# A pooled-attention and snake-activation kernel: the last two token units take two of their seven block products by a second level of Strassen, and GpSimd copies the output weight

## The chip, the cores and the metric

The kernel runs on one core of a Trainium2 chip, in float32 throughout. The metric is the device time of one execution in microseconds. Before the change three executions took 903.77, 904.64 and 906.18 us; their median is 904.64 us.

## The reference

```python
k_p = k.reshape(B, H, Sp, pool, D).mean(axis=3)      # B 8, H 8, S 576, D 64, pool 8
v_p = v.reshape(B, H, Sp, pool, D).mean(axis=3)
attn = softmax(scale * q @ k_p^T)                    # 1e-9 is added to the sum
x = (attn @ v_p).transpose(0, 2, 1, 3).reshape(4608, 512)
h = x @ w_in                                         # 512 x 2048
s = sin(alpha * h)
g = h + s * s / (alpha + 1e-9)
out = g @ w_out                                      # 2048 x 512
```

Nearly all of the arithmetic is in the two matrix products around the sine.

## The kernel before

**Units and groups.** The 4608 tokens are cut into nine units of 512. `run` walks them (u = 0 to 8) and calls `hidden(u, x)`, which makes h and g of one unit; in units 0 to 6 the attention of the next batch (batches 1 to 7) is woven in between. After the last unit, `outputs` computes the second product, eight batches one after the other. A unit has four groups (J = 0 to 3) of 512 hidden columns.

**The first product** is a 2 by 2 block Strassen scheme of seven products (Winograd's form). In the code product p multiplies `self.A[p]`, a block or a sum of blocks of `w_in` (`a..` are blocks, `as..` are sums), by a block of x (`xT`, tile `home0` to `home2`) or a difference of such blocks (`bt`, tile `home3`). One product of one group is `product(...)` at line 834: four matmuls of 128 rows, 128 weights and 256 columns, since two row tiles (`jj`) have two steps (`kk`) each. The trace has two records for each float32 matmul, so eight records for a product. The seven products of a group go in the order 1, 5, 6, 2, 7, 3, 4, and their intermediate sums are kept in four banks of PSUM: 1 goes into b1, ScalarE copies b1 to b6 (line 810), 5 goes into b5, which ScalarE copies out to the tile `p5`; 6 is added onto b6, ScalarE copies b6 to b7, 2 is added onto b1, 7 onto b7, 3 onto b6, 4 onto b7. In between VectorE adds `p5` to b7 and to b6 (line 809; the results are two quarters of the tile `h`), and product 4 may only go onto b7 when VectorE has read it.

**Sine and square.** `sin` (line 984) and `square` (line 991) run on ScalarE, per quarter of the group: quarter (0,0) comes from b1, (1,1) and (0,1) from the sums in `h`, (1,0) from b7 after product 4. `finish` (line 1036) adds the squares on VectorE, and `store_g` sends the group to the DRAM tensor `g_bridge`. The sines of the last two quarters, their squares and `finish` belong to the next group's time (`last_sines`, slots 0 to 2).

**The order is written by hand.** `hidden` has 28 slots to a unit, seven to a group, one for each product. `carry(u)` and `run` fill a list `x[slot]` of further work, and `extras` emits it in the middle of that slot. The five engines each take their instructions in the emitted order, so that a waiting instruction holds up all behind it on its engine.

**Inner products.** In units 1 to 6 three of the products of a unit (5 of groups 2 and 3, 1 of group 3) are themselves done by seven multiplications of 128 columns (`inner_product`, line 1014), in four steps a, b, d, e with two, two, one and two multiplications. After step a ScalarE copies the first result to both halves of a row tile (line 1018) and the second one to SBUF (line 1020); after step b it makes one copy inside the bank (line 1024); after step d VectorE adds the second result of step a (line 1029), and step e adds onto what VectorE wrote. Units 7 and 8 have none.

**The output weight.** In units 7 and 8 `load_w_out` brings `w_out` in and makes its own Strassen operands. It is a generator, and each `next(w)` in `run` is one piece: eight pieces of two ScalarE copies each (line 703), four pieces of four VectorE differences (line 712), five calls of `inner_w` of four VectorE differences each (line 730). In unit 7 the pieces are in slots 9 to 23, in unit 8 in slots 6, 10, 13, 14, 17 and 20. The last group of unit 8 also holds the first steps of `outputs` (slots 22, 25, 27): the first inner products of batch 0 with their VectorE sums (line 1267) and ScalarE copies (lines 1415, 1440).

Of the kernel before, what the change touches and what calls it, by code (L numbers as in the profile page):

```python
# [13 lines left out]
F32 = mybir.dt.float32  # L14
# [26 lines left out]
class Kernel:  # L41
# [637 lines left out]
    def load_w_out(self, wp):  # L679
# [4 lines left out]
        src = self.w_out.rearrange("(k p) n -> p k n", p=P)  # L684
        self.W = {}
        self.wb = {p: wp.tile([P, self.NJ, 2, 2, P], F32, name=f"wb{p}") for p in range(1, 8)}
        flat = lambda t: t[:].rearrange("p a b c d -> p (a b) (c d)")
        b11, b21, b22, t4, t1, t2, b12 = (flat(self.wb[p]) for p in range(1, 8))

# [8 lines left out]
        def put(i, k):  # L698

            for j, t in enumerate(((b11, b12), (b21, b22))[i]):  # L700
                yield
                for n in range(2):
                    nc.scalar.copy(out=t[:, k:k + 4, n * P:(n + 1) * P].rearrange("p k (a c) -> p k a c", a=4),
                                   in_=raw[i, k][:, :, j, :, n, :])
        yield from put(0, 0)
        yield from put(1, 0)
        for c in range(0, kk, 2):
# [9 lines left out]
            tt(t4, b21, t2)  # L717
            if c == 2:
                yield from put(1, 4)
        for p in (1, 2, 4, 6, 7):  # L720
            yield
            self.inner_w(p, wp)
        yield

    def inner_w(self, p, wp):
# [5 lines left out]
        if p in (4, 6, 7, 5):  # L731
            J = (4, 6, 7, 5).index(p)
            t1, t2, t4 = (self.A[i][:, :, J * JW * P:(J + 1) * JW * P].rearrange("p k (j d) -> p k j d", j=2) for i in (1, 2, 3))
        else:
            e = wp.tile([P, 3, 2, 2, P], F32, name=f"we{p}")
# [266 lines left out]
    def inner_product(self, G, p, ps, y):  # L1002
# [29 lines left out]
            products((3, 4), (c[1], c[2]))  # L1032
        return SimpleNamespace(a=a, b=b, d=d, e=e)

    def finish(self, Q, parts=(0, 1)):
        add = lambda o, x, y: self.nc.vector.tensor_tensor(out=o, in0=x, in1=y, op=OP.add)  # L1036
# [15 lines left out]

    def end_hidden(self):
        nc, Q = self.nc, self.group
        self.last_sines(Q, 2)
        self.squares(Q, 0)
        self.squares(Q, 1)
        self.finish(Q)
        self.store_g(Q)
# [405 lines left out]
    def run(self):  # L1465
        nc, tc = self.nc, self.tc
        pool = lambda s, n, b, **kw: s.enter_context(tc.tile_pool(name=n, bufs=b, **kw))
        with ExitStack() as top:
# [10 lines left out]
            with ExitStack() as one:  # L1479
# [35 lines left out]
                for u in range(self.NU):  # L1515
                    x = self.carry(u)
                    if u == self.B - 1:
                        att.close()
                        wo = pool(top, "wo", 1, side="right")
                        self.gp = pool(top, "gp", 1, side="right")  # L1520
                        w = self.load_w_out(wp=wo)
                        next(w)
                        for i in (9, 10, 12, 13, 15, 16, 17, 18, 20, 21, 23):
                            x[i].append(lambda: next(w))
                    elif u > self.B - 1:
                        homes.close()
# [12 lines left out]
            self.op = pool(top, "op", 1, reuse_waits="tile")  # L1539
# [39 lines left out]
```

## Time and profile before

The profiled execution spans 902.6 us from its first to its last instruction; the median of the three runs is 2.0 us above that.

| | busy in 902.6 us | in unit 7 (412.0 to 460.3 us) | in unit 8 (460.3 to 508.3 us) |
|---|---|---|---|
| TensorE matmul (PE) | 895.0 | 48.3 of 48.3 | 48.0 of 48.0 |
| VectorE (DVE) | 677.4 | 23.6 | 37.0 |
| ScalarE (ACT) | 448.3 | 40.5 | 31.6 |
| GpSimd (POOL) | 210.5 | 0.0 | 0.0 |

The columns are busy microseconds. A busy time is the union of the engine's instructions, and instructions of one engine overlap at their ends: four squares in a row, of 0.51, 0.50, 0.71 and 0.71 us, take 2.13 us together. What an instruction costs its engine is therefore the distance of two starts, not its length. From about 508 us on TensorE alternates between unit 8 and the output product, and from about 515 us only the output product is left.

### The profile page before, as it was taken

To read this page: it belongs to the slowest core of one execution; us is meant where nothing else is said; L and a number is where in the kernel's file an instruction comes from. 1 tells how busy PE (TensorE), PEld (TensorE's weight loads), DVE (VectorE), ACT (ScalarE), POOL (GpSimd) and SP (SyncE) were. 2 spreads that over 40 slices of the span, in tenths; PEclk is the share of its full clock that TensorE was granted. 3 is DMA by queue.
4 is the path that set the end of the run, shared out by engine and by line. 5 is a ranking of instruction groups with operands and counts; after the bars stand their busy time and mean duration, and the time that the engine had idled before them with its cause. 6 is when DMAs were issued, how large, how long until landed. Compare 5 with 4: busy or idle time off the path is not lost.

```text
span 902.6 us, 17941 instructions
## 1 busy us (share of the span) xinstructions
PE 895.0 (99%) x7014; PEld 815.8 (90%) x7014; DVE 677.4 (75%) x1011; ACT 448.3 (50%) x1070; POOL 210.5 (23%) x216
## 2 busy tenths in 40 slices
PE   8999999999999999999999999999999999999998
PEld 5787888888888888888888999999999999999997
DVE  7685766768577685764458799979798888889895
ACT  5696776877768778687976611111111111111111
POOL 4788552824438253430000000000000000000000
PEclk9999999999999999999999999999999999999999
DMA  9965867759586595648216346261618162534401
GB/s 261 245 200 158 220 163 202 196 167 251 139 213 186 177 230 143 176 146 293 93 72 227 102 141 199 59 194 38 224 27 230 33 197 67 172 92 127 137 15 40
DMA packets 128747, 141.13 MB, mean 156 GB/s; under 512 B 46920, under 2 KB 95704, under 8 KB 128664
## 3 DMA queue, kind: packets, MB, share of 16 engines
q1 hardware_dynamic: 125880, 137.88, 53.2%
q10 hardware_dynamic: 2784, 2.11, 0.9%
q8 instruction: 56, 0.92, 0.4%
q14 instruction: 27, 0.22, 0.1%
HBM read 75.37 MB, written 47.19 MB: 136 GB/s over the span
## 4 chain that ended last, share of the span: by engine, by line
PE 91%; DMA 3%; DVE 2%; POOL 2%; SPq 1%; issue 0%; ACT 0%; DVEq 0%; POOLq 0%
PE PS L834 42%; PE PS L1312 41%; PE PS L1014 3%; PE PS L308 2%; PE PS L600 2%; DMA a<-in_moe_w_in_dram 2%; DMA kvin<-in_v_dram 1%; SPq L669 1%; PE PS L613 1%; DVE x L1267 1%; DMA h<-in_k_dram 1%; POOL kvin L131 0%; POOL as L675 0%; DVE s L1267 0%; POOL ex L365 0%
## 5 line engine op out<-in xcount | busy, mean ns | idle before, releaser
L834 PE MATMUL PS<-home,a 128*128 128x256 f32 x1104 | 257.9, 381 | 0.7 <-ACT home L527 0.5
L834 PEld LDWEIGHTS PS<-home,a 128*128 128x128 f32 x1104 | 205.2, 190 | 34.1 <-issue 5.0
L834 PE MATMUL PS<-home,as 128*128 128x256 f32 x768 | 183.0, 382 | 0.0
L834 PEld LDWEIGHTS PS<-home,as 128*128 128x128 f32 x768 | 141.6, 190 | 19.8 <-ACT PS L810 1.2
L1312 PE MATMUL PS<-s,wb 128*128 128x144 f32 x896 | 119.1, 286 | 0.0
L1362 POOL TENSOR_TENSOR cc<-cc,cb 128x576 f32<-128x576 f32 x1 | 2.0, 1976 | 501.8 <-DVE cb L1267 501.8
L1312 PEld LDWEIGHTS PS<-s,wb 128*128 128x128 f32 x896 | 113.7, 190 | 0.1
L991 ACT ACTIVATE s<-s,c 128x256 f32<-128x256 f32 (+1 forms) x228 | 113.5, 564 | 0.0
L809 DVE TENSOR_TENSOR h<-PS,p 128x512 f32<-128x512 f32 x72 | 49.2, 683 | 64.2 <-PE PS L834 36.3
L131 POOL TENSOR_TENSOR kvin<-kvin 96x768 f32<-96x768 f32 (+3 forms) x42 | 71.6, 1705 | 69.5 <-DMA kvin<-in_v_dram 67.9
L1440 ACT COPY PS<-PS 128x144 f32<-128x144 f32 x56 | 14.7, 263 | 145.0 <-PE PS L1312 135.5
L984 ACT ACTIVATE s<-h,al 128x256 f32<-128x256 f32 x144 | 65.6, 510 | 39.4 <-DVE h L809 39.3
L1312 PE MATMUL PS<-r,wb 128*128 128x144 f32 x512 | 73.3, 286 | 0.3 <-DVE r L1267 0.3
L1312 PE MATMUL PS<-s,a 128*128 128x144 f32 x512 | 73.2, 286 | 0.0
L1036 DVE TENSOR_TENSOR h<-PS,s 128x512 f32<-128x512 f32 x36 | 24.7, 687 | 59.8 <-ACT s L991 59.8
L984 ACT ACTIVATE s<-PS,al 128x256 f32<-128x256 f32 x144 | 60.1, 470 | 18.6 <-PE PS L834 17.7
L1312 PEld LDWEIGHTS PS<-r,wb 128*128 128x128 f32 x512 | 67.1, 190 | 0.5 <-DVE r L1267 0.5
L1312 PEld LDWEIGHTS PS<-s,a 128*128 128x128 f32 x512 | 67.1, 190 | 0.0
L810 ACT COPY PS<-PS 128x512 f32<-128x512 f32 x72 | 41.5, 576 | 35.0 <-PE PS L834 30.4
L1460 ACT COPY PS<-PS 128x144 f32<-128x144 f32 x56 | 14.7, 263 | 88.1 <-PE PS L1312 88.1
L1312 PE MATMUL PS<-s,we 128*128 128x144 f32 x384 | 54.9, 286 | 0.0
L1312 PE MATMUL PS<-x,wb 128*128 128x144 f32 x384 | 54.9, 286 | 0.0
(215 smaller groups left out, 1407.7 us busy)
## 6 DMA issues: line engine op xcount, KB each, us to landing
g_bridge<-h SPq DMA_DIRECT2D x72, 512.0 KB
r<-g_bridge SPq DMA_DIRECT2D x31, 1152.0 KB
out_dram<-o SPq DMA_DIRECT2D x122, 72.0 KB
kvin<-in_k_dram SPq DMA_DIRECT2D x14, 576.0 KB
q<-in_q_dram SPq DMA_DIRECT2D x7, 1024.0 KB
kvin<-in_v_dram SPq DMA_DIRECT2D x14, 512.0 KB
aM<-tr SPq DMA_DIRECT2D x54, 92.0 KB
aM<-tr SPq DMA_DIRECT2D x54, 88.0 KB
```

Of the source, the lines that this page charges most:

```text
L131: self.nc.gpsimd.tensor_tensor(out=t[..., 0:w] if w > D else out, in0=t[..., 0:w], in1=t[..., w:2 * w], op=OP.add)
L308: nc.tensor.matmul(ps[e][r0 + r:r0 + r + q.shape[-1], h, :], q[s], kb[s, hp, :], start=True, stop=True)
L600: nc.tensor.matmul(o[r:r + 64], w, x, start=start and i < 2, stop=False, skip_group_check=True)
L809: add = lambda o, x, y: nc.vector.tensor_tensor(out=o, in0=x, in1=y, op=OP.add)
L810: copy = lambda o, x: nc.scalar.copy(out=o, in_=x)
L834: nc.tensor.matmul(ps[:, jj, :], self.A[p][:, kk, f * P:(f + 1) * P], x[:, kk, :], start=(start and n == 0), stop=(kk == 1), skip_group_ch ...
L984: self.nc.scalar.activation(out=G.s[:, i, jj, j, :], in_=src[:, jj], func=AF.Sin, scale=self.al[:, f:f + 1])
L991: self.nc.scalar.activation(out=x, in_=x, func=AF.Square, scale=self.c[:, f:f + 1])
L1014: nc.tensor.matmul(o, W[m][:, G.J - J0], X[m], start=start and n == 0, stop=True, skip_group_check=True)
L1036: add = lambda o, x, y: self.nc.vector.tensor_tensor(out=o, in0=x, in1=y, op=OP.add)
L1312: nc.tensor.matmul(out, W[:, J // 2, J % 2, :], A[:, J, :], start=(start and J == 0), stop=(J == self.NJ - 1), skip_group_check=True)
L1440: nc.scalar.copy(out=x1[:, 0, :], in_=x0[:, 1, :])
```

## The change

Units 7 and 8 call a new function `hidden_late` in place of `hidden`. In it products 1 and 5 of groups J = 1, 2 and 3 are done by seven inner multiplications each (`late_chain`), and their steps are placed between the halves of the products of the group in front; products 1 and 5 of group 0 stay as they were. The weights of these inner products are formed by GpSimd (`late_weights`: four sums of 128 x 128 for each of two products and three groups), into the tiles `we1` and `we2`, which `inner_w` needs later, and into a part of `home0`; `late_weights(3)` is done again in unit 8. A further new function, `late_tiles`, takes the room for them and for the differences of x in `home0` in unit 7 and in four small tiles in unit 8. The differences of x (`late_x`, four for each product) are made by GpSimd, except those of product 5 in unit 7, which are VectorE's. The copy of b5 to `p5` goes from ScalarE to VectorE. The copies of `w_out` go from ScalarE to GpSimd. The order of the `inner_w` calls becomes 4, 6, 1, 2, 7, two of them move a slot later (13 to 14, 14 to 15). The sines and squares of quarter (0,1) are done in the group's own slots, so `end_hidden` has two sines and two squares less.

```diff
@@ load_w_out
+        self.we = {p: wp.tile([P, 3, 2, 2, P], F32, name=f"we{p}") for p in (1, 2)}
...
-                    nc.scalar.copy(out=t[:, k:k + 4, n * P:(n + 1) * P].rearrange("p k (a c) -> p k a c", a=4),
+                    nc.gpsimd.tensor_copy(out=t[:, k:k + 4, n * P:(n + 1) * P].rearrange("p k (a c) -> p k a c", a=4),
                                    in_=raw[i, k][:, :, j, :, n, :])
...
-        for p in (1, 2, 4, 6, 7):
+        for p in (4, 6, 1, 2, 7):
             yield
             self.inner_w(p, wp)
@@ new functions
+    def late_weights(self, J, ps=(1, 5)):
+        for p in ps:
+            n = (1, 5).index(p)
+            w = self.w3[n] if J == 3 else self.we[J][:].rearrange("p a b c d -> p (a b c d)")[:, n * 512:n * 512 + 512].rearrange("p (i m) -> p i m", i=4)
+            A = self.A[p][:].rearrange("p k (J j m) -> p k J j m", j=2, m=P)[:, :, J]
+            L = lambda i, j: A[:, j, i]
+            s1, s2, s3, s4 = (w[:, i] for i in range(4))
+            self.sums(((s1, L(1, 0), L(1, 1), OP.add), (s2, s1, L(0, 0), OP.subtract), (s3, L(0, 0), L(1, 0), OP.subtract), (s4, L(0, 1), s2, OP.subtract)))
+            self.WL[p, J] = {1: L(0, 0), 2: L(0, 1), 3: s4, 4: L(1, 1), 5: s1, 6: s2, 7: s3}
+    def late_x(self, u, p, eng=None):
+        x, out = (self.bt[u][:, 0], self.x2[1]) if p == 5 else (self.xT[u][:, 0:2, 0:TH], self.x2[0])
+        R = lambda i, j: x[:, i, j * P:(j + 1) * P]
+        t1, t2, t3, t4 = (out[:, i * P:(i + 1) * P] for i in range(4))
+        for o, a, b in ((t1, R(0, 1), R(0, 0)), (t2, R(1, 1), t1), (t3, R(1, 1), R(0, 1)), (t4, R(1, 0), t2)):
+            (eng or self.nc.gpsimd).tensor_tensor(out=o, in0=a, in1=b, op=OP.subtract)
+        self.XL[p] = {1: R(0, 0), 2: R(1, 0), 3: R(1, 1), 4: t4, 5: t1, 6: t2, 7: t3}
+    def late_chain(self, G, p, ps, y, first):
+        nc = self.nc
+        W, X = self.WL[p, G.J], self.XL[p]
+        c = [ps[:, i, h * P:(h + 1) * P] for i in range(2) for h in range(2)]
+        f = ps.rearrange("p i (h t) -> p i h t", h=2)
+        m5 = self.m5[:, int(p == 5)]
+        def products(ms, outs, start=False):
+            for n, (m, o) in enumerate(zip(ms, outs)):
+                nc.tensor.matmul(o, W[m], X[m], start=start and n == 0, stop=True, skip_group_check=True)
+        def a():
+            products((1, 5), (y[:, 0], y[:, 1]), first)
+            nc.scalar.copy(out=f[:, 0], in_=y[:, 0:1].to_broadcast([P, 2, P]))
+            nc.scalar.copy(out=m5, in_=y[:, 1:2])
+        def b():
+            products((6, 2), (c[1], c[0]))
+            nc.scalar.copy(out=c[2], in_=c[1])
+        def d():
+            products((7,), (c[2],))
+            x = ps.rearrange("p i t -> p (i t)")[:, P:3 * P].rearrange("p (i t) -> p i t", i=2)
+            nc.vector.tensor_tensor(out=f[:, :, 1], in0=x, in1=m5.to_broadcast([P, 2, P]), op=OP.add)
+        def e():
+            products((3, 4), (c[1], c[2]))
+        return SimpleNamespace(a=a, b=b, d=d, e=e)
+    def hidden_late(self, u, extra):
...
+            G.g = self.hp.tile([P, 2, JW, 2, TH], F32, name="h")
+            old = u < self.NU - 1 and J == 0
+            if J == 0:
+                if old:
+                    self.last_sines(Q, 2)
+                else:
+                    sin(Q, 1, 0, Q.b7)
+                extras(0)
+                product(G, 1, G.b1, start=True)
+                copy(G.b6[:], G.b1[:])
+                if old:
+                    self.squares(Q, 0)
+                self.squares(Q, 1)
+                extras(1)
+                product(G, 5, G.b5, start=True)
+                self.finish(Q)
+                self.store_g(Q)
+                G.p5 = self.tp.tile([P, JW, TH], F32, name="p5")
+                nc.vector.tensor_copy(out=G.p5[:], in_=G.b5[:])
+            else:
+                sin(Q, 1, 0, Q.b7)
+                extras(0)
+                extras(1)
+            steps = iter(())
+            if N:
+                y = self.psum([P, 4, P], N.banks[1])
+                c1, c5 = (self.late_chain(N, p, ps, y[:, i:i + 2], i == 0) for p, ps, i in ((1, N.b1, 0), (5, N.b5, 2)))
+                steps = iter((c1.a, c5.a, c1.b, c5.b, c1.d, c5.d, c1.e, c5.e))
+            def chain():
+                f = next(steps, None)
+                if f:
+                    f()
+                if N and f is c1.e:
+                    copy(N.b6[:], N.b1[:])
+            halves = (0, 1), (2, 3)
+            behind = J == 0
+            extras(2)
+            product(G, 6, G.b6, halves[0])
+            if not behind:
+                chain()
+            product(G, 6, G.b6, halves[1])
+            copy(G.b7[:], G.b6[:])
+            if not behind:
+                chain()
+            if J:
+                self.squares(Q, 1)
+            extras(3)
+            product(G, 2, G.b1, halves[0])
+            chain()
+            product(G, 2, G.b1, halves[1])
+            sin(G, 0, 0, G.b1)
+            chain()
+            if J:
+                self.finish(Q)
+                self.store_g(Q)
+            square(G, 0, 0)
+            extras(4)
+            product(G, 7, G.b7, halves[0])
+            chain()
+            product(G, 7, G.b7, halves[1])
+            add(G.g[:, 1, :, 1], G.b7[:], G.p5[:])
+            chain()
+            sin(G, 1, 1, G.g[:, 1, :, 1])
+            extras(5)
+            product(G, 3, G.b6, halves[0])
+            chain()
+            product(G, 3, G.b6, halves[1])
+            add(G.g[:, 0, :, 1], G.b6[:], G.p5[:])
+            chain()
+            sin(G, 0, 1, G.g[:, 0, :, 1])
+            square(G, 0, 1)
+            add(G.g[:, 0, :, 0], G.b1[:], G.s[:, 0, :, 0])
+            extras(6)
+            product(G, 4, G.b7, halves[0])
+            if behind:
+                chain()
+            product(G, 4, G.b7, halves[1])
+            if behind:
+                chain()
+            if N:
+                N.p5 = self.tp.tile([P, JW, TH], F32, name="p5")
+                nc.vector.tensor_copy(out=N.p5[:], in_=N.b5[:])
@@ end_hidden
         nc, Q = self.nc, self.group
-        self.last_sines(Q, 2)
-        self.squares(Q, 0)
+        self.sin(Q, 1, 0, Q.b7)
@@ run
+                        self.WL, self.XL = {}, {}
                         w = self.load_w_out(wp=wo)
                         next(w)
+                        self.late_tiles(u)
                         for i in (9, 10, 12, 13, 15, 16, 17, 18, 20, 21, 23):
                             x[i].append(lambda: next(w))
+                        self.late_weights(1, (1,))
+                        self.late_x(u, 1)
+                        x[0].append(lambda: self.late_weights(1, (5,)))
+                        x[1].append(lambda: self.late_x(7, 5, nc.vector))
+                        x[4].append(lambda: self.late_weights(2))
+                        x[6].append(lambda: self.late_weights(3))
                     elif u > self.B - 1:
                         homes.close()
                         self.gq = pool(top, "gq", 1, side="right")
-                        for i in (6, 10, 13, 14, 17, 20):
+                        self.late_tiles(u)
+                        for i in (6, 10, 14, 15, 17, 20):
                             x[i].append(lambda: next(w))
+                        x[0].append(lambda: self.late_x(8, 1))
+                        x[0].append(lambda: self.late_x(8, 5))
+                        x[6].append(lambda: self.late_weights(3))
                         x[5].append(lambda: self.load_g(0, ("r11", "r12", "r22")))
                         for i, f in zip((23, 25, 25, 27), self.inner_w(5, None)):
                             x[i].append(f)
                         o = self.outputs()
                         for i in (22, 25, 27):
                             x[i].append(lambda: next(o))
-                    self.hidden(u, x)
+                    (self.hidden if u < self.B - 1 else self.hidden_late)(u, x)
                 self.end_hidden()
             self.gs = pool(top, "gs", 1, reuse_waits="tile")
             self.op = pool(top, "op", 1, reuse_waits="tile")
```

More of the change, by code (lines that the diff above doesn't have):

```diff
@@ L734, in inner_w @@
         else:
-            e = wp.tile([P, 3, 2, 2, P], F32, name=f"we{p}")
+            e = self.we[p] if p in self.we else wp.tile([P, 3, 2, 2, P], F32, name=f"we{p}")
             t1, t2, t4 = (e[:, i] for i in range(3))
@@ L1033, in inner_product, with late_tiles @@
         return SimpleNamespace(a=a, b=b, d=d, e=e)
+    def late_tiles(self, u):
+        if u < self.NU - 1:
+            t = self.home(0, [P, self.K1, 2 * TH])
+            t = [t[:, i] for i in range(4)]
+            m5 = self.we[2][:].rearrange("p a b c d -> p (a b c d)")[:, 1024:1280]
+        else:
+            t = [self.gq.tile([P, self.NJ, self.T], F32, name=f"s{i}0")[:].rearrange("p a b -> p (a b)")[:, 0:4 * P] for i in range(4)]
+            m5 = self.gq.tile([P, self.NJ, self.T], F32, name="s01")[:].rearrange("p a b -> p (a b)")[:, 0:2 * P]
+        self.m5 = m5.rearrange("p (a b c) -> p a b c", a=2, b=1)
+        self.x2 = t[:2]
+        self.w3 = [x.rearrange("p (i m) -> p i m", i=4) for x in t[2:]]
@@ new lines, in hidden_late, with group, product, extras @@
+    def hidden_late(self, u, extra):
+        nc = self.nc
+        add = lambda o, x, y: nc.vector.tensor_tensor(out=o, in0=x, in1=y, op=OP.add)
+        copy = lambda o, x: nc.scalar.copy(out=o, in_=x)
+        sin, square = self.sin, self.square
+        def group(J, banks):
+            b1, b6, b5, b7 = (self.psum([P, JW, TH], i) for i in banks)
+            return SimpleNamespace(u=u, J=J, b1=b1, b5=b5, b6=b6, b7=b7, banks=banks, g=None, s=self.s, p5=None, early=True)
+        def product(G, p, ps, part=range(4), start=False):
+            xT, bt = self.xT[u], self.bt[u]
+            B = lambda i, j: xT[:, 2 * i:2 * i + 2, j * TH:(j + 1) * TH]
+            x = {1: B(0, 0), 2: B(1, 0), 3: B(1, 1), 4: bt[:, 3], 5: bt[:, 0], 6: bt[:, 1], 7: bt[:, 2]}[p]
+            for n in part:
+                jj, kk = divmod(n, 2)
+                f = G.J * JW + jj
+                nc.tensor.matmul(ps[:, jj, :], self.A[p][:, kk, f * P:(f + 1) * P], x[:, kk, :],
+                                 start=(start and n == 0), stop=(kk == 1), skip_group_check=True)
+        for J in range(self.NJ):
+            def extras(k):
+                for f in extra[7 * J + k]:
+                    f()
+            Q = self.group
+            if J == 0:
+                if u < self.NU - 1:
+                    banks = [(self.turn + 1 + i) % 5 for i in range(4)]
+                    self.turn = (self.turn + 4) % 5
+                    self.sets = banks, [5, 6, 7, (self.turn + 1) % 5]
+                G = group(0, self.sets[0])
+                N = group(1, self.sets[1])
+            else:
+                G = self.next
+                q = Q.banks
+                N = group(J + 1, (q[2], q[1], q[0], q[3])) if J < self.NJ - 1 else None
+            self.before, self.group, self.next = Q, G, N
+            if u == self.NU - 1 and not N:
+                self.turn, self.aturn = self.sets[1][3], 2
+            G.g = self.hp.tile([P, 2, JW, 2, TH], F32, name="h")
+            old = u < self.NU - 1 and J == 0
+            if J == 0:
+                if old:
+                    self.last_sines(Q, 2)
+                else:
+                    sin(Q, 1, 0, Q.b7)
[11 more added lines that the diff above has]
+                nc.vector.tensor_copy(out=G.p5[:], in_=G.b5[:])
+            else:
+                sin(Q, 1, 0, Q.b7)
[9 more added lines that the diff above has]
+                if f:
+                    f()
+                if N and f is c1.e:
[48 more added lines that the diff above has]
+                nc.vector.tensor_copy(out=N.p5[:], in_=N.b5[:])
```

## The prediction

> **What bounds the kernel now.** I read the page first, then the busy time of the two units that change, then the order of time on TensorE, VectorE and ScalarE in them, then the groups by shape in the middle units, which already hold inner products. The page:
>
> ```profile
> span 902.6 us, 17941 instructions
> PE 895.0 (99%) x7014; PEld 815.8 (90%) x7014; DVE 677.4 (75%) x1011; ACT 448.3 (50%) x1070; POOL 210.5 (23%) x216
> ```
>
> The busy time in units 7 and 8 (stretch, length, then busy us of PE, PEld, DVE, ACT, POOL; PEclk; DMA):
>
> ```profile
> 412.00:460.30 48.30, 48.30 (x225) 42.52 (x224) 23.55 (x34) 40.52 (x91) 0.00 (x0) 1.00 0.45 162
> 460.30:508.30 48.00, 48.00 (x225) 42.24 (x224) 37.01 (x56) 31.61 (x68) 0.00 (x0) 1.00 0.47 162
> ```
>
> The reader is to see that TensorE has no gap in these 96 us and runs at clock 1.00, so only fewer TensorE cycles shorten them, and every wait that the change brings costs its full length. From 515 us the output product goes on as densely, so nothing behind pays a lost microsecond back, with one exception below.
>
> **The saving.** TensorE's order of time, first plain products of unit 7 (16 records), then inner multiplications in unit 6:
>
> ```profile
> 418.49 3.62 PE L834 MATMUL PS<-home,as 128*128 128x256 f32 x16
> 421.94 3.62 PE L834 MATMUL PS<-home,a 128*128 128x256 f32 x16
> ...
> 400.94 0.38 PE L1014 MATMUL PS<-ex,q 128*128 128x128 f32 x2
> 401.16 0.39 PE L1014 MATMUL PS<-home,as 128*128 128x128 f32 x2
> 401.39 0.39 PE L1014 MATMUL PS<-last,q 128*128 128x128 f32 x2
> 401.61 0.60 PE L834 MATMUL PS<-home,a 128*128 128x256 f32 x2
> ```
>
> From start to start, 16 records take 3.45 us: 1.726 us for a plain product, 0.863 for half of one. One inner multiplication (two records) takes 0.223, so two of them 0.445, and a product by seven 1.56. That saves 0.17 us for each product. Two products of three groups in two units are twelve: 12 x 0.17 = 2.05 us. This is all that can be gained: 0.23% of the time, less than the 0.3% that a measurement of this kernel can tell from no change. All depends on whether the steps wait.
>
> **What the steps need.** Prices come from start to start where the trace shows a series, plus 0.03 to 0.06 us from an engine's end to the next engine's start and 0.14 from ScalarE's copy to TensorE; TensorE's result is there 0.2 us after its last record's slot. Inner copies and add, and VectorE and ScalarE in the two units:
>
> ```profile
> L1029 DVE TENSOR_TENSOR PS<-PS,m 128x256 f32<-128x256 f32 x18 | 7.8, 433 | 23.7 <-PE PS L1014 23.7
> L1018 ACT COPY PS<-PS 128x256 f32<-128x256 f32 x18 | 6.7, 375 | 5.0 <-DVE PS L1029 4.9
> L1020 ACT COPY m<-PS 128x128 f32<-128x128 f32 x18 | 5.0, 276 | 0.0
> L1024 ACT COPY PS<-PS 128x128 f32<-128x128 f32 x18 | 4.5, 250 | 11.9 <-PE PS L1014 11.9
> L131 POOL TENSOR_TENSOR kvin<-kvin 128x512 f32<-128x512 f32 x6 | 9.4, 1560 | 0.5
> ```
>
> ```profile
> 458.26 1.22 DVE L1036 TENSOR_TENSOR h<-h,s 128x1024 f32<-128x1024 f32 x1
> 459.39 2.62 DVE L712 TENSOR_TENSOR wb<-wb,wb 128x512 f32<-128x512 f32 x4
> ```
>
> ```profile
> 455.50 2.13 ACT L991 ACTIVATE s<-s,c 128x256 f32<-128x256 f32 x4
> 458.46 0.57 ACT L810 COPY PS<-PS 128x512 f32<-128x512 f32 x1 [0.84 <-PE PS L834]
> ```
>
> ScalarE gets 2 x (0.375 + 0.276 + 0.250) = 1.8 us a group and loses the `p5` copy (0.59) and, in unit 7, 16 copies of `w_out` at 0.62: it stays under 36 of 46 us, so its load is no bound, only its order. VectorE gets six adds of 0.43 and four `p5` copies of 0.69 (line 281 copies that shape in 0.69) in a unit; unit 8 then has 37.0 + 5.3 = 42.3 of 46 us, and there the queue matters. I walked each group along the three queues; four places come out late.
>
> *First to second group (both units).* In the first group the steps lie late, and the copy of b1 to b6 stands on ScalarE behind two sines and two squares that wait for product 3. From the end of product 3: result 0.2, VectorE's add 0.69, sines 0.82, squares 0.81, copy 0.57, hand-overs 0.17: 3.26 us. TensorE meanwhile has step d, half a product, step e, half a product, step e: 2.84. It waits 0.42, and after a wait the trace's second record takes 0.10 more. 0.52 x 2 = 1.0 us. What hid the copy before was product 5, 1.73 us, which stood behind it.
>
> *Third group of unit 7.* From the start of product 6: ScalarE has step a's second copies at about 3.3 us, then squares of 512 columns (0.61 each, 0.71 the last) to 4.65. `finish` waits for them: 0.61 + 1.13 on VectorE; behind it slot 18's four `w_out` differences, 2.5 us, and only then step d's add, 0.43. Sum 9.4. TensorE reaches step e of product 1 after three and a half products and steps a, a, b, b, d, d: 8.26. Wait 1.13, with the restart 1.23.
>
> *Third group of unit 8.* The same place, and what stands ahead are the `inner_w` calls of slots 14, 15 and 17: 12 differences x 0.63 = 7.6 us. VectorE is free about 0.2 before product 6 starts, so it reaches `finish` at 7.4 instead of 4.65, the add ends at 9.6, the wait is 1.37, with the restart 1.47.
>
> *Last group of unit 8.* It has only five products now, but VectorE's work is the same and `p5` more. From the end of product 3 of the group before, VectorE has two adds (1.2), `inner_w` (2.5), `p5` (0.6), four sums of the output product (2.8, from 503.58 to 506.38 in the trace of before), three `inner_w` differences with `finish` (3.6) and the add of b7: 11.6 with hand-overs. TensorE has step e, six products and two multiplications of the output product at 0.98: 11.0. Product 4 waits 0.6. The same add releases four sines and two squares (2.45) that now stand on ScalarE ahead of the output product's copy (0.26): 2.8 us, while TensorE has only product 4, 1.73. Another 1.05. With two restarts 1.9 us. Before, two of these sines and the squares stood behind that copy.
>
> *GpSimd.* It had nothing to do here (0.00 above). Copies on GpSimd are not in the trace. The nearest rows bound one of 128x512 between 0.73 (two inputs of 256 columns, line 131's shortest) and 1.56 (two inputs of 512, above); I take 1.04, a product of 512 with a repeated input. The 24 sums and differences ahead of the copies cost 0.45 to 0.95 each (line 794's rows); I take 0.74. Twelve copies are needed by the differences of slot 18: 24 x 0.74 + 12 x 1.04 = 30.2 us from the unit's start. VectorE comes to them at 27.4 + 6.4 = 33.8 us (two groups of 15.7 and 11.7 us, then `finish`). 3.6 us are to spare: nothing. The lower ends give 19.6. The upper ends give 41.5, 7.7 us late, and all of it would fall on TensorE, since step d's add stands behind. DMA issues don't move to another queue.
>
> One thing speaks against GpSimd beside VectorE: line 1036's add of 1024 columns takes 1.22 us with GpSimd idle and 1.53 in the mean of the middle units. The Trainium skill (SBUF — State Buffer, "SBUF: two separate sides") says why: a VectorE instruction with two SBUF inputs and a GpSimd instruction exclude each other for the whole instruction. By that rule, an estimate, the five such instructions of unit 7's third group would wait a copy each if GpSimd were still at work then, some 5 us more; by the row's 0.31 each it is 1.6. My sum has neither, for GpSimd is through by then. As to the copy itself, the Trainium skill (GPSIMD Engine Reference, "Engine selection") calls a one-input instruction about line-rate, which would put it at the low end; by that the sum is the same.
>
> *Given back.* At 536.85 us TensorE waits 0.42 us for VectorE in the output product, with the restart 0.52. Arriving later it may wait less: between 0 and 0.5 back; I take 0.3.
>
> **The sum.** -2.05 + 1.0 + 1.23 + 1.47 + 1.9 - 0.3 = +3.25 us. The profiled execution would span 902.6 + 3.25 = 905.9. Runs lie about 2.0 above the span, so the median 904.64 becomes 907.9 us, 0.36% slower.
>
> **The rivals.** *The cover holds.* Each wait comes out of a queue walked with mean prices. If VectorE ends step d's add before 8.2 us into both third groups, 1.2 to 1.4 us ahead of my walk, and is as far ahead in the last group, only the first-to-second waits stay: -2.05 + 1.0 = -1.05, 903.6. If those go too, 902.6. For it speaks that ScalarE and VectorE have idle time in every group; against it that VectorE's late adds stand behind work in emitted order, which idle time elsewhere doesn't help. *GpSimd late.* From 33.8 us after unit 7's start every microsecond of GpSimd's delay is one of TensorE's: up to +7.7 on the forecast, 910 to 915.6. For it: POOL rows of 0.95 and 1.56 when VectorE is busy. Against it: VectorE is half idle in unit 7. *The copies win.* That taking 9.9 us of copies off ScalarE shortens anything: ScalarE wasn't waited for (PE 48.30 of 48.30), so this gives nothing, 904.6 less at most the saving.
>
> **How the numbers follow.** The forecast, waits of 3.5 to 7 us in sum: 0.62; it covers 905.8 to 909.6, and three tenths of it lie within 0.3% (up to 907.35), 0.19. The cover holds: 0.20, within 0.3%. GpSimd late: 0.15, slower. Otherwise than any of these, a real gain: 0.03. So slower 0.43 + 0.15 = 0.58, same 0.39, faster 0.03. The range goes from 903.6, which leaves out about half of the cover's case, to 912.0, about half of GpSimd's: no more than 0.2 in all.
>
> **What would show it.** In unit 7 and 8 the matmul line of the inner steps waits for VectorE's inner add once in each third group, 1.1 to 1.5 us, and nowhere else over 0.2; product 6 of the second group waits 0.3 to 0.5 for ScalarE's copy; product 4 and product 7 of the output's first multiplication wait 0.5 and 1.0; GpSimd's copies end before 33 us into unit 7. If the two units are 94 us long with no waits, the walk is wrong; if VectorE's `w_out` differences wait for GpSimd, the price of the copy is.

## The result, and the profile after

| | before | changed | ratio, 95% interval |
|---|---|---|---|
| first comparison, median (lowest to highest) | 905.13 us (903.77 to 906.18, 5 runs) | 909.35 us (908.26 to 911.08, 5 runs) | 1.0049 [1.0036, 1.0062] |
| second comparison (`changed_again`) | 906.07 us (17 runs) | 908.95 us (907.46 to 910.36, 12 runs) | 1.0033 [1.0020, 1.0046] |
| profiled execution: span | 902.6 us | 909.3 us | |

The changed kernel is slower by 0.33 to 0.49%, 3 to 4 us. First the page of the changed kernel, its span and the busy time of each engine:

```profile
span 909.3 us, 18214 instructions
...
PE 895.6 (98%) x7086; PEld 816.1 (90%) x7086; DVE 691.8 (76%) x1035; ACT 444.1 (49%) x1082; POOL 243.9 (27%) x276
```

TensorE's busy time has hardly moved (895.0 before), yet the span is 6.7 us longer. So TensorE stands still somewhere. The busy time in units 7 and 8 (stretch, length, busy us of PE, PEld, DVE, ACT, POOL; PEclk; DMA) says where:

```profile
412.00:460.30 48.30, 47.20 (x281) 40.85 (x273) 28.39 (x46) 33.24 (x88) 23.76 (x44) 1.00 0.49 175
460.30:508.30 48.00, 46.67 (x255) 41.40 (x254) 36.58 (x57) 31.87 (x80) 9.02 (x16) 1.00 0.46 156
```

Before, PE was 48.30 of 48.30 and 48.00 of 48.00. The clock is still 1.00, POOL has got its work, and PE has gaps. TensorE's order of time shows each of them (start, duration, engine, line, operation, operands; in brackets the idle time and what ended it):

```profile
435.21 1.13 PE L1117 MATMUL PS<-home,as 128*128 128x256 f32 x4 [0.16 <-ACT PS L1103]
...
456.52 0.49 PE L1079 MATMUL PS<-home,home 128*128 128x128 f32 x2 [0.94 <-DVE PS L1093]
...
505.85 0.38 PE L1079 MATMUL PS<-home,s 128*128 128x128 f32 x1 [1.17 <-DVE PS L1093]
...
518.94 1.99 PE L1117 MATMUL PS<-home,a 128*128 128x256 f32 x8 [0.48 <-DVE h L1102]
...
521.65 1.25 PE L1499 MATMUL PS<-s,wb 128*128 128x144 f32 x8 [0.72 <-ACT PS L1627]
```

The bracket counts from the modelled end of the record in front, which lies 0.16 us after its slot. The loss is read better from start to start: the step into the waiting record less the usual step (0.216 us for 256 columns, 0.110 for 128). In order these are 0.327, 1.105, 1.329, 0.639 and 0.880 us, the first twice (once in each unit), and the second record after each wait comes 0.104 later than usual. A further step, at 427.14, loses 0.07, and five more lose 0.03 each.

Why the second one waits, from VectorE's order of time in the third group of unit 7:

```profile
451.77 0.69 DVE L1224 TENSOR_TENSOR h<-PS,s 128x512 f32<-128x512 f32 x1 [2.16 <-ACT s L992]
452.38 1.22 DVE L1224 TENSOR_TENSOR h<-h,s 128x1024 f32<-128x1024 f32 x1
453.51 2.61 DVE L713 TENSOR_TENSOR wb<-wb,wb 128x512 f32<-128x512 f32 x4
456.04 0.42 DVE L1093 TENSOR_TENSOR PS<-PS,we 128x256 f32<-128x256 f32 x1
```

`finish` waits 2.16 us for ScalarE's squares; four `w_out` differences stand behind it, and only then comes the add that TensorE's step e needs (456.46 to 456.52). In unit 8, twelve `inner_w` differences stand ahead of `finish` instead; the last of them, `finish` and the add:

```profile
503.03 0.68 DVE L731 TENSOR_TENSOR we<-wb,we 128x512 f32<-128x512 f32 x1
503.63 0.68 DVE L1224 TENSOR_TENSOR h<-PS,s 128x512 f32<-128x512 f32 x1
504.23 1.21 DVE L1224 TENSOR_TENSOR h<-h,s 128x1024 f32<-128x1024 f32 x1
505.37 0.42 DVE L1093 TENSOR_TENSOR PS<-PS,s 128x256 f32<-128x256 f32 x1
```

ScalarE's order of time shows the first and the last wait:

```profile
432.97 0.91 ACT L985 ACTIVATE s<-h,al 128x256 f32<-128x256 f32 x2 [1.43 <-DVE h L1102]
433.79 0.89 ACT L992 ACTIVATE s<-s,c 128x256 f32<-128x256 f32 x2
434.58 0.58 ACT L1103 COPY PS<-PS 128x512 f32<-128x512 f32 x1
...
518.92 1.71 ACT L985 ACTIVATE s<-h,al 128x256 f32<-128x256 f32 x4 [3.90 <-DVE h L1102]
520.53 0.89 ACT L992 ACTIVATE s<-s,c 128x256 f32<-128x256 f32 x2
521.33 0.27 ACT L1627 COPY PS<-PS 128x144 f32<-128x144 f32 x1
```

The copy of b1 to b6 stands behind two sines and two squares and ends at 435.16, 0.05 us before product 6; the output's copy stands behind four sines and two squares, and TensorE goes on 0.05 us after it. Before the change that copy stood ahead of the last two sines (ScalarE):

```profile
514.31 0.26 ACT L1440 COPY PS<-PS 128x144 f32<-128x144 f32 x1 [1.44 <-DVE h L809]
514.49 0.91 ACT L984 ACTIVATE s<-h,al 128x256 f32<-128x256 f32 x2
```

**From the waits to the time.** In three pieces, read from the matmul records. The first, the "stretch", goes from the first matmul behind the last batch's attention to multiplication 7 of the output product's first inner product (the third in time). The second goes from there to the last matmul, and the tail from there to the end. The recorded expectations call the stretch's start unit 7's start, but the last three products of unit 6 (5.28 us in every trace) still come first: unit 7's own first matmul is at 416.76 us before and 419.60 us in the changed kernel. So the windows 412.0 to 460.3 and 460.3 to 508.3 hold the end of unit 6 and leave out the end of unit 8.

| kernel | stretch begins | stretch | to the last matmul | tail |
|---|---|---|---|---|
| before | 411.48 | 103.94 | 382.61 | 4.61 |
| changed | 414.32 | 107.33 | 382.22 | 5.42 |

The change acts in the second and third column: +3.39 - 0.39 = +3.00 us. The 2.84 us ahead of the stretch aren't put down to it: in the twelve traces of the study the stretch begins anywhere between 411.1 and 414.3 us, in the changed kernel's second trace at 412.7, and in a kernel with the same early part (`copies_back_on_scalar`) at 411.2. The three traces with the old `hidden` lie at 411.1 to 412.1, so a small part of it may belong to the change; that isn't shown. The tail is 4.6 to 5.5 us in these kernels; why was not followed up. In the changed kernel's two traces it is 5.42 and 5.41, 0.8 longer than before. That the stretch happened to begin late in the one profiled execution is why the two spans differ by more than the times do.

### The profile page after: what moved, and what is told of

It is laid out like the page before. It is cut to its first block, busy times and chain, and to the rows that moved or that the text cites. A ratio compares the mean times of both kernels' runs of the same rounds, so it can differ in the third digit from the quotient of the medians.

```text
span 909.3 us, 18214 instructions
## 1 busy us (share of the span) xinstructions
PE 895.6 (98%) x7086; PEld 816.1 (90%) x7086; DVE 691.8 (76%) x1035; ACT 444.1 (49%) x1082; POOL 243.9 (27%) x276
## 4 chain that ended last, share of the span: by engine, by line
PE 91%; DVE 3%; ACT 2%; POOL 1%; DMA 1%; issue 1%; SPq 0%; DVEq 0%; POOLq 0%
PE PS L1499 42%; PE PS L835 33%; PE PS L1117 6%; PE PS L1015 3%; PE PS L308 2%; PE PS L600 2%; PE PS L1079 1%; PE PS L613 1%; DMA q<-in_q_dram 1%; POOL kvin L131 1%; DMA h<-in_k_dram 1%; ACT s L992 1%; DVE h L1224 1%; DVE h L1102 0%; ACT s L985 0%
## 5 line engine op out<-in xcount | busy, mean ns | idle before, releaser
L835 PE MATMUL PS<-home,a 128*128 128x256 f32 x848 | 199.9, 382 | 1.8 <-DVE h L810 1.3
L835 PEld LDWEIGHTS PS<-home,a 128*128 128x128 f32 x848 | 156.7, 190 | 28.7 <-issue 5.0
L835 PE MATMUL PS<-home,as 128*128 128x256 f32 x576 | 138.9, 383 | 0.0
L835 PEld LDWEIGHTS PS<-home,as 128*128 128x128 f32 x576 | 105.2, 190 | 14.8 <-ACT PS L811 1.2
L131 POOL TENSOR_TENSOR kvin<-kvin 96x768 f32<-96x768 f32 (+3 forms) x42 | 73.6, 1752 | 72.3 <-DMA kvin<-in_v_dram 70.6
L810 DVE TENSOR_TENSOR h<-PS,p 128x512 f32<-128x512 f32 x56 | 38.1, 680 | 44.6 <-PE PS L835 28.3
L1224 DVE TENSOR_TENSOR h<-h,s 128x1024 f32<-128x1024 f32 x36 | 55.4, 1538 | 0.9 <-ACT s L992 0.9
```

What stands on the lines that cost most here:

```text
L131: self.nc.gpsimd.tensor_tensor(out=t[..., 0:w] if w > D else out, in0=t[..., 0:w], in1=t[..., w:2 * w], op=OP.add)
L810: add = lambda o, x, y: nc.vector.tensor_tensor(out=o, in0=x, in1=y, op=OP.add)
L835: nc.tensor.matmul(ps[:, jj, :], self.A[p][:, kk, f * P:(f + 1) * P], x[:, kk, :], start=(start and n == 0), stop=(kk == 1), skip_group_ch ...
```

## The experiments

All timed comparisons are against the kernel before. The last column compares stretch, output product and tail with the 491.15 us of the kernel before. A kernel with one run has no interval, and its trace is what it is judged by.

| kernel | time, us (runs) | ratio, 95% interval | stretch | to last matmul | by the trace |
|---|---|---|---|---|---|
| `copies_on_gpsimd` | 905.05 (10) | 0.9994 [0.9981, 1.0006] | 103.94 | 382.61 | -0.02 |
| `changed_again` | 908.95 (12) | 1.0033 [1.0020, 1.0046] | 107.33 | 382.22 | +3.81 |
| `differences_behind` | 907.85 (10) | 1.0021 [1.0007, 1.0034] | 105.75 | 382.22 | +2.23 |
| `b6_copy_ahead` | 908.75 (1) | | 106.48 | 382.22 | +2.49 |
| `last_sines_behind` | 907.31 (1) | | 106.45 | 382.37 | +2.81 |
| `copies_back_on_scalar` | 909.62 (1) | | 109.79 | 382.22 | +5.46 |
| `copies_four_times` | 935.67 (1) | | 134.18 | 382.22 | +30.68 |
| `copies_twice` | 918.91 (1) | | 117.65 | 382.22 | +14.18 |
| `before_copies_four_times` | 924.73 (1) | | 124.64 | 382.61 | +20.65 |
| `all_waits_moved` | 904.20 (12) | 0.9983 [0.9973, 0.9993] | 102.21 | 383.32 | -0.68 |

The theory: the inner products save about 2 us of TensorE's slots, and six waits, each from the place of one step in VectorE's or ScalarE's queue, take 5.2. The rivals: the copies on GpSimd do it, or VectorE and GpSimd get in each other's way.

### The copies alone

The kernel before, with this alone:

```diff
-                    nc.scalar.copy(out=t[:, k:k + 4, n * P:(n + 1) * P].rearrange("p k (a c) -> p k a c", a=4),
+                    nc.gpsimd.tensor_copy(out=t[:, k:k + 4, n * P:(n + 1) * P].rearrange("p k (a c) -> p k a c", a=4),
```

> The kernel before with one part of the change alone: the 16 copies of w_out on GpSimd. My theory (only waits in the three queues count): nothing, 904 to 906 us, no gap in TensorE's order from 412 to 508 us; GpSimd is busy 9 us and through before the differences of slot 15. Rival 'GpSimd beside VectorE': VectorE's two-input instructions of the eighth unit get longer and TensorE waits 1 us or more. Rival 'something early': the first 70 us get longer by 2 to 3 us, as the changed kernel's trace shows (its eighth unit starts 2.8 us later than before); then unit 7 starts at 414 here too.

The ratio is 0.9994 [0.9981, 1.0006] and the stretch 103.94, as before, with no gap from 412 to 508 us. The copies by themselves neither gain nor cost. That isn't for lack of contention. GpSimd's copies and VectorE's adds in unit 7:

```profile
418.30 6.96 POOL L703 COPY wb<-wb 128x512 f32<-128x512 f32 x8 [24.77 <-ACT s L984]
425.21 4.51 POOL L703 COPY wb<-r 128x512 f32<-128x512 f32 x8
```

```profile
418.90 1.09 DVE L804 TENSOR_TENSOR home<-home 128x512 f32<-128x512 f32 x1
...
422.55 1.68 DVE L1036 TENSOR_TENSOR h<-h,s 128x1024 f32<-128x1024 f32 x1
...
433.83 1.22 DVE L1036 TENSOR_TENSOR h<-h,s 128x1024 f32<-128x1024 f32 x1
```

Eight copies take 4.5 us undisturbed and 6.96 beside these adds; the 1024-column add takes 1.68 beside copies and 1.22 alone. Each waits for about one instruction of the other, and TensorE had room for it.

### The copies back on ScalarE

The changed kernel with that line put back.

> The changed kernel with the copies of w_out back on ScalarE. My theory: the six waits of the changed kernel (5.05 us with restarts) stay as they are, and ScalarE, with 8.5 us of copies more in unit 7, makes the inner steps wait in the second and third group: two to three further waits of 0.3 to 1.8 us, 911 to 913 us. Rival 'GpSimd beside VectorE is the cost': the waits for VectorE in unit 7 shrink and the kernel gets 1 to 3 us faster than the changed one.

All six waits stay within 0.01 us, and new ones come: 1.59 at 447.83, 0.33 at 462.50, 0.23 at 466.28, each with its restart; the stretch grows by 2.46 to 109.79. TensorE, then ScalarE, around the largest:

```profile
447.83 0.49 PE L1079 MATMUL PS<-home,as 128*128 128x128 f32 x2 [1.42 <-ACT we L1084]
```

```profile
446.19 1.12 ACT L704 COPY wb<-r 128x512 f32<-128x512 f32 x2
447.21 0.36 ACT L1083 COPY PS<-PS 128x256 f32<-128x256 f32 x1
447.51 0.26 ACT L1084 COPY we<-PS 128x128 f32<-128x128 f32 x1
```

With inner products in ScalarE's queue, two copies of `w_out` (1.0 us) stand ahead of step a's. So the move to GpSimd, worth nothing alone, is worth 2.5 us beside the other half of the change. The single time (909.62, where 911 to 913 were expected) doesn't show it, since the stretch began 3.1 us earlier in this execution than in the changed kernel's first trace and the tail was 0.8 us shorter; the stretch does.

### The third groups: differences behind the add

```diff
-                        for i in (9, 10, 12, 13, 15, 16, 17, 18, 20, 21, 23):
+                        for i in (9, 10, 12, 13, 15, 16, 17, 19, 20, 21, 23):
...
-                        for i in (6, 10, 14, 15, 17, 20):
+                        for i in (6, 10, 14, 15, 19, 20):
```

> The changed kernel with one piece of w_out work in each unit moved behind the steps d: slot 18 to 19 in unit 7 and slot 17 to 19 in unit 8. My theory: the two waits of the third groups (1.10 + 0.10 and 1.33 + 0.10) vanish; the last group of unit 8, whose VectorE queue now has four differences more ahead, waits up to 0.8 longer; 1.8 to 2.6 us faster than the changed kernel. Rival 'finish itself comes too late, whatever stands behind it': both waits stay within 0.3 us and the time is the changed kernel's.

Both waits for L1093 are gone: their cause is the `w_out` and `inner_w` differences ahead of it. But the differences moved in unit 8 now lie nearer the last group, and TensorE's order of time there is:

```profile
515.82 1.99 PE L1117 MATMUL PS<-home,a 128*128 128x256 f32 x8 [1.33 <-DVE h L1102]
518.53 1.25 PE L1499 MATMUL PS<-s,wb 128*128 128x144 f32 x8 [0.71 <-ACT PS L1627]
```

Product 4's wait grows from 0.64 to 1.49, and the output's first multiplication loses 0.11 and a restart to the `p5` copy (L1221). Of 2.64 us taken away, 1.06 come back: 107.33 - 105.75 = 1.58, less than the 1.8 to 2.6 expected, for the `p5` copy wasn't foreseen.

### The first-to-second groups: the copy of b1 ahead of the sines

The sines and squares that stood ahead of the copy go to the next group:

```diff
-            sin(G, 0, 1, G.g[:, 0, :, 1])
-            square(G, 0, 1)
+            if not behind:
+                sin(G, 0, 1, G.g[:, 0, :, 1])
+                square(G, 0, 1)
...
             if behind:
                 chain()
+                sin(G, 0, 1, G.g[:, 0, :, 1])
...
+            if J == 1:
+                square(Q, 0, 1)
             if J:
                 self.squares(Q, 1)
```

> The changed kernel with one edit: in the first group of both units the copy of b1 to b6 stands on ScalarE ahead of the two sines and two squares, and the squares go behind the next group's. My theory: the two waits of 0.33 us with their restarts of 0.10 vanish and the four others stay: 106.5 us from unit 7's start to the output product's seventh multiplication, against 107.3. Rival 'the copy is late because step e is late on TensorE': the waits stay.

Both waits of 0.327 are gone, the other four are unchanged, and the stretch is 0.85 shorter: 2 x (0.327 + 0.104) = 0.86. The cause is what stands ahead of the copy on ScalarE.

### The last group: two sines and two squares behind the output's copy

```diff
-            sin(G, 0, 1, G.g[:, 0, :, 1])
-            square(G, 0, 1)
+            if N or u < self.NU - 1:
+                sin(G, 0, 1, G.g[:, 0, :, 1])
+                square(G, 0, 1)
@@ end_hidden
+        self.sin(Q, 0, 1, Q.g[:, 0, :, 1])
+        self.square(Q, 0, 1)
         self.sin(Q, 1, 0, Q.b7)
```

> The changed kernel with one edit: two sines and two squares of the last group of unit 8 go behind the output product's copy on ScalarE, as before the change. My theory: the wait of 0.88 us with its restart of 0.10 in front of the output product's seventh multiplication vanishes, that of product 4 (0.64) stays: 106.3 us instead of 107.3. Rival 'that copy waits for VectorE': it stays.

```profile
516.18 1.99 PE L1117 MATMUL PS<-home,a 128*128 128x256 f32 x8 [0.48 <-DVE h L1102]
518.01 1.14 PE L1502 MATMUL PS<-s,wb 128*128 128x144 f32 x8
```

TensorE's order of time: product 4 still waits for VectorE's add (0.64), the multiplication at 518.01 no longer waits. 0.88 us less in the stretch; 0.15 of it is spent again later, where TensorE waits 0.18 at 539.76 in the output product.

### Is GpSimd near a limit?

In the changed kernel GpSimd's copies stand in 431.66 to 440.61:

```profile
431.66 4.49 POOL L704 COPY wb<-wb 128x512 f32<-128x512 f32 x8
436.11 4.50 POOL L704 COPY wb<-r 128x512 f32<-128x512 f32 x8
```

They are through 21.0 us after unit 7's own first matmul. To see when they would hurt, they were made four times (then twice, and four times in the kernel before with copies on GpSimd):

```diff
-                for n in range(2):
+                for n in (0, 1) * 4:
```

> The changed kernel with each GpSimd copy of w_out made four times, 64 copies of 0.56 us start to start. My theory (GpSimd costs nothing until it is late for the differences, then one for one): the 32 copies that slot 15's differences need end about 18 us into the copies, 449.6 us on the changed kernel's scale, 2.7 us after VectorE wants to start them, and those of slot 18 about 458.5 instead of 453.5; with the exclusion on top TensorE waits 6 to 18 us more in unit 7, at VectorE's step d or at product 4, and unit 8 is unchanged. Rival 'GpSimd's work is hidden whatever its length': no more than 1 us.

It cost far more than either theory allowed. GpSimd, then VectorE, of `copies_four_times`:

```profile
429.39 17.86 POOL L704 COPY wb<-wb 128x512 f32<-128x512 f32 x32
447.19 17.88 POOL L704 COPY wb<-r 128x512 f32<-128x512 f32 x32
```

```profile
437.76 0.69 DVE L1224 TENSOR_TENSOR h<-PS,s 128x512 f32<-128x512 f32 x1 [4.25 <-ACT s L992]
438.37 27.77 DVE L1224 TENSOR_TENSOR h<-h,s 128x1024 f32<-128x1024 f32 x1
466.06 0.42 DVE L1093 TENSOR_TENSOR PS<-PS,we 128x256 f32<-128x256 f32 x1
```

One add that takes 1.22 us alone took 27.77: until the last of GpSimd's copies was through (465.07) and 1.07 more. The copies kept their pitch of 0.56 us all along, so they gave way to nothing. The instructions of VectorE ahead of it, with an input in PSUM, ran at their usual 0.69 beside the copies. Behind the add stands the inner add of step d, and TensorE waited 25.2 us, in the second group, not for the late `w_out` differences that I had thought of. Two more runs asked whether this is the rule, since in `copies_on_gpsimd` the same add had got through after one copy:

> The changed kernel with each w_out copy on GpSimd made twice: 32 copies, about 17.9 us from 18 us after unit 7's start. In copies_four_times one VectorE instruction with two SBUF inputs (the 1024-column add of the second group) stood 27.8 us, until the last copy was through. Theory A, a VectorE instruction that comes up while GpSimd works back to back gets nothing until GpSimd pauses: the add comes up about 9 us ahead of the last copy and stands some 9 us; TensorE waits about 7 us at step e of the second group of unit 7, and from unit 7's first matmul to the output product's 7th multiplication it takes 113.5 to 116.5 us instead of 107.33. Theory B, it waits for one copy only and something else held it in copies_four_times: the add takes under 1.9 us, and the stretch takes 107.3 to 108.3 us.

> The kernel before with the w_out copies on GpSimd, each made four times: 64 copies, 36 us from about 6 us after unit 7's start. In copies_on_gpsimd VectorE's 1024-column add came up in the middle of the copies and took 1.68 us, 0.46 more than alone: it waited for one copy, and the next copy waited for it. Theory A (nothing until GpSimd pauses): here an add stands until the last copy, 15 to 32 us, and TensorE waits 10 us or more. Theory B (one copy each, as in copies_on_gpsimd): no VectorE instruction takes over 2.3 us, and the time is within 2 us of copies_on_gpsimd but for the w_out differences, which wait for the last copies: up to 5 us more on TensorE.

`copies_twice`, VectorE:

```profile
438.11 9.95 DVE L1224 TENSOR_TENSOR h<-h,s 128x1024 f32<-128x1024 f32 x1
```

As theory A has it: it stands until the copies end at 446.99. It ends 8.73 us late, and TensorE waits 7.36, so 1.37 us of delay are hidden there. The stretch came out above the range, at 117.65, since 2.97 us more went into matmuls at half the clock after the wait (below). `before_copies_four_times` shows both cases in one kernel. VectorE, then the busy time around the two adds (the last two columns are the DMA's busy share and GB/s):

```profile
421.61 1.58 DVE L1036 TENSOR_TENSOR h<-h,s 128x1024 f32<-128x1024 f32 x1
...
432.89 23.63 DVE L1036 TENSOR_TENSOR h<-h,s 128x1024 f32<-128x1024 f32 x1
```

```profile
417.00:424.00 7.00, 7.00 (x35) 6.15 (x34) 5.68 (x6) 4.62 (x11) 6.66 (x8) 1.00 1.05 392
432.00:442.00 10.00, 7.03 (x33) 5.86 (x31) 9.71 (x2) 2.96 (x7) 10.00 (x20) 0.97 0.00 0
```

The first add was in after one copy, as theory B has it; the second stood until the copies ended at 455.45, and TensorE waited 18.3 us. So neither theory holds alone. Wherever an add got in after one copy, transfers were running (share 1.05 here, 1.04 in 417 to 423 us of `copies_on_gpsimd`); wherever it was shut out, none were (0.00 here and in the other two kernels). Whether the transfers decide it wasn't tried, and stays open. Idle transfers alone don't shut VectorE out. In unit 8 of the changed kernel, while GpSimd makes sums of two inputs without a pause and the share is 0.00 (471.3 to 472.2 us), VectorE's 512-column add at 471.29, with both inputs in SBUF, got in after one sum: it took 0.94 us instead of 0.69, and the next sum 0.90 instead of 0.45. All three shut-outs were beside copies.

### All waits moved

The three edits of order together, with the last group's `p5` copy on ScalarE and the last `inner_w` call's differences later:

```diff
-                N.p5 = self.tp.tile([P, JW, TH], F32, name="p5")
-                nc.vector.tensor_copy(out=N.p5[:], in_=N.b5[:])
+                N.p5 = self.tp.tile([P, JW, TH], F32, name="p5")
+                (copy if u == self.NU - 1 and J == self.NJ - 2 else nc.vector.tensor_copy)(N.p5[:], N.b5[:])
...
-                        for i, f in zip((23, 25, 25, 27), self.inner_w(5, None)):
+                        for i, f in zip((26, 26, 26, 27), self.inner_w(5, None)):
```

> The changed kernel with the order mended at all six places: the copy of b1 to b6 ahead of the sines in the first group, the two pieces of w_out work of the run before, the last p5 copy on ScalarE, the inner_w differences of product 5 behind the add of b7, two sines and two squares of the last group behind the output product's copy. My theory: the saving of 2.05 us comes out in units 7 and 8, and TensorE reaches the output product some 5 us earlier than in the changed kernel; there VectorE, busy over nine tenths, is late by about 1 us, so 0.5 to 1.5 us faster than the kernel before: 903.6 to 904.6 us. Rival 'the inner products cost more than their waits': the time stays 1 us or more above the kernel before.

```profile
412.00:460.30 48.30, 48.30 (x285) 42.57 (x280) 28.89 (x46) 33.78 (x89) 23.75 (x44) 1.00 0.48 175
460.30:508.30 48.00, 48.00 (x265) 43.09 (x264) 38.33 (x60) 33.53 (x84) 9.02 (x16) 1.00 0.48 162
```

TensorE's busy time has no gap any more in these windows (busy time by stretch, as above). The stretch is 1.73 us shorter than before. Part of it is given back in the output product, where TensorE now comes early and meets VectorE:

```profile
531.30 1.25 PE L1505 MATMUL PS<-x,wb 128*128 128x144 f32 x8 [0.20 <-DVE x L1460]
...
538.76 1.25 PE L1505 MATMUL PS<-r,wb 128*128 128x144 f32 x8 [0.34 <-DVE r L1460]
```

By start-to-start steps these are 0.36 and 0.50 us, with 0.07 at 520.06 and three restarts. The output product takes 383.32 instead of 382.61. The ratio is 0.9983 [0.9973, 0.9993]: this version is faster than both kernels. Against the one before it gains 1.5 us (0.6 to 2.4 by the interval, 0.7 by the trace); against the changed one, by the two ratios to the one before, 4.5 to 6 (4.5 by the trace). The two weren't run against each other.

## Why the prediction was right

The forecast came about with its mechanism; the rivals didn't. Term by term, in us:

| step of the prediction | predicted | measured | from |
|---|---|---|---|
| the saving | -2.05 | -1.96 | records of the twelve products, below |
| first to second group, two waits | +1.0 | +0.86 | steps; -0.85 in `b6_copy_ahead` |
| third group of unit 7 | +1.23 | +1.21 | 1.105 + 0.104 |
| third group of unit 8 | +1.47 | +1.43 | 1.329 + 0.104 |
| last group: product 4, output's multiplication 7, restarts | +1.9 | +1.73 | 0.639 + 0.880 + 0.21 |
| not foreseen | | +0.23 | step a of product 5 behind the second copy of step a of product 1, in all six groups |
| given back in the output product | -0.3 | -0.49 | 0.42 + 0.10 at 537 gone, 0.04 new at 543.47 |
| sum | +3.25 | +3.01 | +3.00 by the two columns above |

**The saving** was sized right: before, 96 records of 0.2158 take 20.72 us; 168 inner records at 0.111 take 18.65, 2.07 less, and plain records behind inner ones, with steps up to 0.220 instead of 0.216, take 0.11 of it back. What the walk left out is small: in each of the six groups step a of product 5 waits for ScalarE's second copy (L1084) of step a of product 1, once for 0.07 and five times for 0.03. These stay in `all_waits_moved` too, and are why its stretch is 1.73 us shorter and not 1.96.

**The waits** were each at the place and behind the instruction that the walk named, and five of the six were undone by moving just what stood in front: the differences ahead of `finish` or step d's add, the sines ahead of the copy of b1, the sines ahead of the output's copy. The sixth, product 4's in the last group, grew to 1.49 us when four differences more stood ahead of it; it was undone only in `all_waits_moved`, by two edits at once and beside the others. None was off by more than 0.17 us (the last, 0.88 for 1.05). For product 4 the prediction writes six products of TensorE; its 11.0 us is the sum with five, which is what stands there. The upper end of its 3.5 to 7 us of waits, 909.6, leaves out the 0.3 us given back.

**The cover holds** fell: in both third groups the add came as late as walked, although in unit 7 VectorE had 2.16 us of idle time just before `finish`. **The copies win** fell: 0.9994 alone. Only beside the inner products do they gain something: 2.46 us of the stretch, and that against a variant that is neither of the two kernels.

**GpSimd late** did not come about, but not for the reason I gave, and that this term came out at nothing was luck. The instructions ahead of the copies are 28, not 24; they took 0.55 us each in the mean, not 0.74, and began at 414.72, 4.9 us ahead of unit 7's first matmul. A copy repeats every 0.56 us, under my lower bound of 0.73 and far under the 1.04 that I took: the nearest rows were instructions with two inputs, or one input read twice, and a copy has one. (The Trainium skill, GPSIMD Engine Reference, "Engine selection", calls one input about line-rate, which the prediction took for its low end; the measured copy lies below even that.) And the limit isn't the `w_out` differences, which VectorE came to at 453.51, 33.9 us after unit 7's first matmul (33.8 predicted), but the first VectorE instruction with two SBUF inputs that meets the copies, the second group's add of 1024 columns:

```profile
440.03 0.69 DVE L1224 TENSOR_TENSOR h<-PS,s 128x512 f32<-128x512 f32 x1 [4.25 <-ACT s L992]
440.64 1.22 DVE L1224 TENSOR_TENSOR h<-h,s 128x1024 f32<-128x1024 f32 x1
```

In the changed kernel it starts at 440.64, 21.0 us after that matmul, and the last copy is through at 440.61. The 3.6 us "to spare" were 0.03, with the 1.37 us behind the add that `copies_twice` shows hidden. With the prediction's prices from 414.72 on (28 x 0.74 + 16 x 1.04 = 37.4 us) the copies would have ended at 452.1. The add would then have been shut out for some 11 us and TensorE have lost about 10: an estimate, by the behaviour of the three kernels with more copies. As to the page on the SBUF (the Trainium skill, SBUF — State Buffer, "SBUF: two separate sides"), by whose rule the two engines exclude each other for one whole instruction: that fits the adds of 1.58 and 1.68 us, which waited for one copy, and not those of 9.95, 23.63 and 27.77, which waited for all of them.

**The size in time.** The forecast added 3.25 us to 904.64; the changed kernel's medians are 909.35 and 908.95. The kernel before had 905.13 and 906.07 in the same comparisons, so the differences are 4.2 and 2.9 us, around the 3.0 of the trace and up to 0.8 more for the tail, which the forecast didn't have. They lie on both sides of the 3.25.

## What to carry to other kernels

Where one engine has no gap, a saving on it is worth only what the others can keep up with: walk each of their queues in emitted order from the moment of release, and look for long work that was put in front of a short step when nobody waited for that step. Here the walk with durations from the trace found every wait over 0.1 us, each to within 0.2, and the same walk tells the repair: put the filler behind the step, which turned +0.33 to +0.49% into -0.17%. Work handed to an idle engine isn't free for that reason alone: look up what it shares with the engines that aren't idle, and how close its end comes to their next instruction of the kind that shares.

## What the runs showed of the hardware that was not expected

A VectorE add with both inputs in SBUF can be shut out for as long as GpSimd copies back to back: 9.95, 23.63 and 27.77 us for an instruction of 1.22, in three kernels, while the same kind of add got in after one copy in two other places (1.58 and 1.68). In all three cases the DMA engines were idle; beside GpSimd's sums of two inputs an add got in with idle DMA engines too (0.94 us instead of 0.69).

After such a wait TensorE runs slow. The busy time of `copies_four_times` by stretch, the clock third from the end:

```profile
455.00:465.00 10.00, 0.00 (x0) 0.00 (x0) 10.00 (x1) 0.00 (x0) 10.00 (x19) 0.50 0.00 0
465.00:475.00 10.00, 8.46 (x40) 7.50 (x41) 6.80 (x11) 5.37 (x15) 0.07 (x1) 0.76 0.29 107
```

The granted clock falls to 0.50 in the idle time, and the first matmuls behind it step by 0.427 us instead of 0.216. In `copies_twice`, after only 7.4 us of waiting, matmuls ran so from 448.5 to 454.4 us and cost 2.97 us more; in `before_copies_four_times` 2.4. The waits of about 1 us in the changed kernel cost only their restart of 0.104.
